# Exponentials as three shifted bit streams, and an inverse row transform by halves, in a spectral filter beside an attention

## The chip, the cores and the metric

The kernel runs on one core of a Trainium2 chip. Its engines are TensorE (PE; its weight loads are listed apart as PEld), VectorE (DVE), ScalarE (ACT), GpSimd (POOL) and the DMA queues, issued here by SyncE (SP). The metric is the device time of one execution in microseconds; the profile is of one execution.

## The reference

Two independent computations on a 2048 x 640 input each, whose outputs are put side by side. The first is a spectral filter: a two-dimensional real Fourier transform, a product with a complex weight, and the inverse transform. The second is a multi-head attention with 32 heads of width 20.

```python
def _A_ref(x, w_r, w_i):
    X = rfft2(x.astype(float32))
    X = X * (w_r + 1j * w_i)
    return irfft2(X, s=(S, D)).astype(bfloat16)

def _B_ref(x, wqkv, wo):          # H = 32, Dh = 20
    q, k, v = heads(x @ wqkv)
    p = softmax(einsum("bhqd,bhkd->bhqk", q, k) * Dh ** -0.5)
    o = einsum("bhqk,bhkd->bhqd", p, v)
    return merge(o) @ wo
```

All the times of this text belong to a program that does both. The scores of the attention are 32 x 2048 x 2048, and each needs an exponential; the filter is a chain of matrix products with tables of cosines and sines.

## The kernel before

The program is written by a scheduler of its own: at build time it plays the engines through with estimated durations, picks for each engine what to issue next, and emits fixed instruction streams. The engines then run in order and wait for each other on semaphores. So a change of one operation can move every instruction after it.

The scores are computed as tiles of 128 keys x 512 queries of one head (`score_mm`). Head width is 20, padded to 32 rows, so that up to four such matmuls, of four heads, run side by side in the array. There are 32 units (a query block and a group of four heads) of 64 tiles each. Most tiles go in pairs to ScalarE, which takes two PSUM banks in one instruction:

```python
self.put("act", lambda e: e.activation(o, in_, AF.Exp, bias=ACT_BIAS, scale=ACT_SCALE), ...)   # 128 x 1024
```

The others go to VectorE, which forms the exponential from the bits of a half-precision number. The scores come scaled so that 1024 steps are one power of two, with an offset in them. A first step per tile, clamping and converting to a 16-bit integer, frees the PSUM bank; three more steps run on four tiles at once.

```python
# p1, per tile: PSUM fp32 -> int16 (named L946 in the profile)
e.tensor_scalar(o, in_, 0.0, 31744.0, ALU.max, ALU.min)
...
# per batch of four tiles, on 2048 columns (L974, L975, L976)
e.tensor_scalar(Gu, Iu, 0x3FF, 0x3800, ALU.bitwise_and, ALU.bitwise_or)   # p2
e.tensor_tensor(Gf, If, Gf, ALU.mult)                                     # p3
e.tensor_scalar(Iu, Iu, 0x7C00, 0x0008, ALU.bitwise_and, ALU.bitwise_or)  # p4, in place
```

G and I, read as half-precision numbers, are two terms whose sum is the exponential, and TensorE adds them by multiplying both with the values. There are two such buffer pairs.

The value matmuls (`try_pv`, L1053) have 32 output rows, so four heads run side by side; a VectorE tile needs two of them, a ScalarE tile one. The filter's stages, S1 to S4, and the projections run between as background jobs, released by time between FT0 and FT1. `keep` matmuls are issued where TensorE would otherwise idle.

The eight PSUM banks: two pairs for ScalarE, four for everything else.

The inverse row transform (S3) before the change has four tables of 8 x 128 x 512, cosines and sines of two halves of the output rows, for even and odd frequencies:

```python
for idx in range(4):                 # h: half of the rows, par: even or odd frequencies
    h, par = divmod(idx, 2)
    for pl in range(2):
        for lt in range(3):
            for n in range(8):       # four cosine, four sine blocks
                e.matmul(o, l, self.tabs[b][:, n, :], start=(n == 0), stop=(n == 7))
            # one eviction, 128 x 512, to bf16
            e.tensor_scalar(Z[..., h * 512:(h + 1) * 512], ps, sc, None, ALU.mult)
```

The last stage (S4) multiplies Z with a table G, 192 matmuls of 320 columns, and writes sums and differences out.

Of the kernel before, what the change touches and what calls it, by code (L numbers as in the profile page):

```python
# [255 lines left out]
S = 2048  # L256
# [5 lines left out]
OFF = 15360.0  # L262
QSCALE = (DH ** -0.5) * math.log2(math.e) * 1024.0
LN2 = math.log(2.0)
PC = 1.50702
ACT_SCALE = LN2 / 1024.0
ACT_BIAS = math.log(PC) - 15.0 * LN2
SUM_MIN = 192.0
FBC = 322
UNITS = ([(qc, g) for g in range(4) for qc in range(2)] + [(0, g) for g in range(4, 8)] + [(1, g) for g in range(4, 8)]  # L270
# [4 lines left out]
class Job:  # L275
    def __init__(self, name, prio, pe=(), ev=(), after=(), rel=0.0, post=None):
        self.name = name
        self.prio = prio
        self.pe = list(pe)
        self.ev = list(ev)  # L280
        self.after = list(after)
        self.rel = rel
        self.post = post
        self.bank = None
        self.hold = 0
        self.rdy = []
        self.nxt = 0
        self.enx = 0
        self.done = False
        self.seq = 0  # L290
        self.need = []


class KB:
# [44 lines left out]
    def alloc(self):  # L339
# [11 lines left out]
        self.Gb = []  # L351
        for _ in range(2):
            self.i1_off = a.take(4096)
            self.Ib.append(a.bf(self.i1_off, 2048))
            self.Gb.append(a.bf(a.take(4096), 2048))
        self.Of = [a.f32(a.take(2048), 512) for _ in range(2)]
# [26 lines left out]
        assert self.zend - zB >= 24576 and self.zend - zD >= 5200, (self.zend - zB, self.zend - zD)  # L383
# [13 lines left out]
    def alloc_filter(self):  # L397
        a = self.ar
        zA, zB, zC, zD = self.zA, self.zB, self.zC, self.zD
        self.xf = [a.bf(zA + 10240 * i, 8 * 640).rearrange("p (t d) -> p t d", t=8) for i in range(2)]  # L400
        self.ftmp = [a.f32(zD + 2560 * i, 640) for i in range(2)]
        self.fx = [a.bf(o, 1280) for o in (zC + 13312, self.ob_off, self.wo_off)]
        self.xs = [self.nc.dram_tensor("xs%d" % i, (1024, 640), BF16, kind="Internal").ap() for i in range(2)]
        self.tabs = [a.bf(zC + 8192 * i, 8 * 512).rearrange("p (t k) -> p t k", t=8) for i in range(2)]
        self.X1 = a.bf(zB, 5 * 2 * 1024).rearrange("p (c r k) -> p c r k", c=5, r=2)
        self.Y = a.bf(zA, 8 * 4 * FBC).rearrange("p (c m l) -> p c m l", c=8, m=4)
        self.FD = a.bf(zC, 4 * 3 * FBC).rearrange("p (m t l) -> p m t l", m=4, t=3)
        o = zC + 4 * 3 * FBC * 2
        self.Wb = [[a.bf(o + (2 * i + s) * 2 * FBC * 2, 2 * FBC).rearrange("p (r l) -> p r l", r=2) for s in range(2)] for i in range(2)]
        self.Wx = [[a.bf(zA + 2576 + (2 * i + s) * 2 * FBC * 2, 2 * FBC).rearrange("p (r l) -> p r l", r=2) for s in range(2)] for i in range(2)]  # L410
        self.TU = a.bf(zD, 4 * FBC).rearrange("p (s r l) -> p s r l", s=2, r=2)
        self.VX = a.bf(zD + 8 * FBC, 4 * FBC).rearrange("p (s r l) -> p s r l", s=2, r=2)
        self.X24 = a.bf(zD + 16 * FBC, 8)
        self.Z = a.bf(zB, 3 * 4 * 1024).rearrange("p (t m s) -> p t m s", t=3, m=4)
        self.G = a.bf(zA, 3 * 2 * 640).rearrange("p (t m d) -> p t m d", t=3, m=2)
        self.outB += [a.bf(o, 640) for o in (zC + 5888, zC + 7168)]
        self.T1 = [a.f32(zA + 7680 + 1280 * i, 320) for i in range(2)]
        self.yo = [[a.bf(zA + 10240 + 2560 * i + 1280 * s, 640) for s in range(2)] for i in range(2)]
# [78 lines left out]
    def setup_B(self):  # L497
# [52 lines left out]
        off2 = float(np.uint32(0x44A044A0).view(np.float32))  # L550
# [410 lines left out]
    def close_batch(self):  # L961
        b = self.dbatch % 2
        tiles = self.dtiles
        n = len(tiles)
        self.dtiles = []
        self.dbatch += 1
        self.batches_open[b] = n * 2
        I_ = self.Ib[b][:, 0:n * 512]
        G_ = self.Gb[b][:, 0:n * 512]
        Iu, Gu = I_.bitcast(U16), G_.bitcast(U16)  # L970
        If, Gf = I_.bitcast(F16), G_.bitcast(F16)
        ik = [("I", b, i) for i in range(n)]
        ops = [
            (lambda e, en: e.tensor_scalar(Gu, Iu, 0x3FF, 0x3800, ALU.bitwise_and, ALU.bitwise_or), 100 + 0.26 * 512 * n, ik, [("G", b), ("G2", b)], [], "p2"),  # L974
            (lambda e, en: e.tensor_tensor(Gf, If, Gf, ALU.mult), 125 + 0.52 * 512 * n, ik + [("G", b)], [("G2", b)], [], "p3"),  # L975
            (lambda e, en: e.tensor_scalar(Iu, Iu, 0x7C00, 0x0008, ALU.bitwise_and, ALU.bitwise_or), 100 + 0.26 * 512 * n, [("G2", b)], ik, [], "p4"),  # L976
        ]

        def gdone():
            for i, t in enumerate(tiles):  # L980
                self.pv.append(dict(tile=t, src=self.Gb[b].bitcast(F16)[:, i * 512:(i + 1) * 512], key=("G2", b), last=False, b=b, bat=True, sid=1))
            for i, t in enumerate(tiles):
                self.pv.append(dict(tile=t, src=self.Ib[b].bitcast(F16)[:, i * 512:(i + 1) * 512], key=("I", b, i), last=True, b=b, bat=True, sid=2))
        bt = self.bat[self.dbatch - 1]

        def go():
            self.dve_push(ops, gdone, prio=self.PRP)
        bt[1] = (n, go)
        if bt[0] == n:
            go()  # L990
# [5 lines left out]
    def pv_waves(self, u):  # L996
# [7 lines left out]
        for (kt, sid), q in quads.items():  # L1004
            if len(q) == 4:
                ks = [it["key"] for it in q] + [("V", g // 2, kt), ("Vone",), ("Vpad",)]
# [4 lines left out]
    def try_pv(self, nmax=4):  # L1011
# [22 lines left out]
        for it in group:  # L1034
            uu, kt, j = it["tile"]
            rk += [it["key"], ("V", g // 2, kt)]
            hl = 4 * (g % 2) + j
            todo.append((self.V[:, kt, g // 2, hl * 21: hl * 21 + 32], it["src"], j, j not in st))
# [6 lines left out]
        if len(st) == len(group) and all(t[3] for t in todo):  # L1045
            wk, pwk = [("ps", bank)], []
        else:
            wk, pwk = [], [("ps", bank)]

# [215 lines left out]
    def eligible(self, J):  # L1265
# [5 lines left out]
        if J.need and not self.avail(J.need):  # L1271
            return False
# [344 lines left out]
    def filter_tables(self):  # L1617
# [14 lines left out]
        for h in range(2):  # L1632
            for par in range(2):
                k = 2 * np.arange(512, dtype=np.int64) + par
                sh = s[h * 512:(h + 1) * 512]
                ang = th * ((k[:, None] * sh[None, :]) % S)
                c_, n_ = np.cos(ang), np.sin(ang)
                if par == 0:
                    n_[0, :] = alt[h * 512:(h + 1) * 512]
                m = np.concatenate([c_.reshape(4, 128, 512), n_.reshape(4, 128, 512)], 0)  # L1640
                t3.append(m.transpose(1, 0, 2))
# [22 lines left out]
        g = np.stack([cl * np.cos(a4), cl * np.sin(a4)], 1)  # L1664
# [3 lines left out]
    def jobs_A(self, after, need):  # L1668
# [162 lines left out]
        hook("ldt3", S2, lambda: [load_t(self.tabs, self.c_t3, i, 3, "t3", [zr("C", 2)]) for i in range(2)])  # L1831
        S3 = []
        yk = [("Y", kc, m) for kc in range(9) for m in range(2)]
        for idx in range(4):
            h, par = divmod(idx, 2)
            b = idx % 2
            js = []
            for pl in range(2):
                zi = 2 * par + pl
                for lt in range(3):  # L1840
                    M = 128 if lt < 2 else 65
                    pe = []
                    for n in range(8):
                        m = (n // 4) * 3 if pl == 0 else 1 + n // 4

                        def mk(bank, n=n, m=m, lt=lt, M=M, b=b, par=par):
                            o = ps[0:M, bank, :]
                            l = self.Y[:, 4 * par + n % 4, m, lt * 128:lt * 128 + M]
                            r_ = self.tabs[b][:, n, :]
                            return lambda e: e.matmul(o, l, r_, start=(n == 0), stop=(n == 7))  # L1850
                        pe.append((mk, 216.0, yk + [("t3", idx), ("t3b", b), zr("A", 2), zr("C", 3)]))

                    def mkev(bank, zi=zi, lt=lt, M=M, h=h):
                        o = self.Z[0:M, lt, zi, h * 512:(h + 1) * 512]
                        in_ = ps[0:M, bank, :]
                        sc = -1.0 if zi % 2 == 1 else 1.0
                        return lambda e, en: e.tensor_scalar(o, in_, sc, None, ALU.mult)  # L1857
                    ev = [(mkev, 608.0, [zr("B", 2), zr("D", 3)], [("Z", lt, zi, h), zr("B", 1), zr("D", 2)], [], False)]
                    js.append(add(Job("S3", 0.0, pe, ev, after=S2)))
            S3 += js  # L1860
            if idx < 2:
                hook("ldt3_%d" % (idx + 2), js, (lambda idx: lambda: load_t(self.tabs, self.c_t3, idx + 2, 3, "t3", []))(idx))
        hook("ldwo", S3, lambda: [self.dma(self.woL[i][0:80, :], self.B_wo[480 + 80 * i:560 + 80 * i, :], 102400, w=[("woL", i), zr("C", 3)], name="ld_woL") for i in range(2)])
        hook("ldG", S3, lambda: self.dma(self.G.rearrange("p t m d -> p (t m d)"), self.c_G.ap(), 983040, w=[("G",), zr("A", 2)], name="ld_G"))
        for sc in range(8):
            for half in range(2):
                for T in range(2):
                    pe = []
                    for n in range(6):
# [8 lines left out]
                        ks = [("Z", lt, 2 * T + m, sc // 4), ("G",), zr("A", 3), zr("B", 2), zr("D", 3)]  # L1878
# [37 lines left out]
    FT1 = 760000.0  # L1916
# [210 lines left out]
```

## Time and profile before

| | |
|---|---|
| time, median of three | 794.51 us (794.4 to 799.35) |
| span of the profiled execution | 793.0 us |
| granted TensorE clock, mean | 0.999 of full speed |
| exponentials on ScalarE | 822 of two tiles |
| tiles on VectorE | 404 |
| data moved by DMA | 48.66 MB, 61 GB/s in the mean |

How to read it: the page gives each engine's busy time and its share of the span; a group line has the source line, engine and operation, what is written and read with shapes and count, then the busy time and the mean duration of one instruction, then the idle time just before them and what ended most of it. Busy times of overlapping instructions are merged, so count times mean can be more than the busy time. A window line gives the length, each engine's busy time with the number of instructions, the granted clock, the DMA share and GB/s. A timeline line gives start and length in us.

### The profile page before, as it was taken

The numbers are of one execution on the slowest core, as the hardware profiler recorded it, in microseconds if no ns is written. First come the engines' busy times: TensorE is split into PE (matmuls) and PEld (weight loads), VectorE is DVE, ScalarE is ACT, GpSimd is POOL, SyncE is SP. The second block draws the span as 40 slices with busy tenths as digits, with TensorE's granted clock in tenths as the row PEclk, the third lists the DMA queues.
The fourth block names the chain that finished last, engine by engine and source line by source line (L and its number), as shares of the span: only waits on it lengthen the run. The fifth ranks groups of instructions, "written<-read, shape, count | busy, mean of one in ns | idle before, by whom it ended". The sixth has DMA issues, their size and how long they took to land.

```text
span 793.0 us, 15248 instructions
## 1 busy us (share of the span) xinstructions
PE 751.3 (95%) x6115; PEld 235.1 (30%) x6115; DVE 699.7 (88%) x1077; ACT 764.6 (96%) x835; POOL 142.8 (18%) x141
## 2 busy tenths in 40 slices
PE   8999999999999999999999999999999999999897
PEld 4422333333222222223322332222222222332233
DVE  3698998988897888888999999899989998899996
ACT  5899999999999999999999999999999999999995
POOL 7396950000000012003022010001000100000000
PEclk9999999999999999999999999999999999999999
DMA  9023332021145212211011103010200112111101
GB/s 294 26 60 105 93 93 68 22 53 27 45 126 173 74 60 63 70 53 50 18 38 47 53 26 124 13 66 20 72 20 18 41 29 66 52 36 53 34 21 53
DMA packets 42861, 48.66 MB, mean 61 GB/s; under 512 B 16454, under 2 KB 36168, under 8 KB 41760
## 3 DMA queue, kind: packets, MB, share of 16 engines
q1 hardware_dynamic: 42016, 46.32, 19.4%
q0 software_dynamic: 768, 1.32, 0.6%
q8 instruction: 49, 0.80, 0.4%
q14 instruction: 28, 0.23, 0.1%
HBM read 32.53 MB, written 8.36 MB: 52 GB/s over the span
## 4 chain that ended last, share of the span: by engine, by line
ACT 65%; PE 24%; DVE 8%; DMA 1%; SPq 1%; issue 1%
ACT arena L1393 64%; PE ps L812 8%; PE ps L1053 5%; PE ps L634 3%; DVE arena L946 2%; DVE arena L975 2%; PE ps L605 2%; DVE arena L976 1%; DVE arena L974 1%; DMA arena<-ct 1%; PE ps L681 1%; PE ps L1762 1%; PE ps L1199 1%; SPq L471 1%; PE ps L1877 1%
## 5 line engine op out<-in xcount | busy, mean ns | idle before, releaser
L1393 ACT ACTIVATE arena<-ps 128x1024 f16<-128x1024 f32 x822 | 757.4, 1109 | 10.8 <-PE ps L812 8.3
L812 PE MATMUL ps<-arena 32*128 32x512 bf16 x2048 | 325.1, 384 | 27.6 <-ACT arena L1393 22.6
L946 DVE TENSOR_SCALAR arena<-ps 128x512 int16<-128x512 f32 x404 | 269.7, 683 | 44.7 <-PE ps L812 43.0
L1053 PE MATMUL ps<-arena 128*32 128x512 f16 x2452 | 192.4, 385 | 1.9 <-DVE arena L976 1.8
L812 PEld LDWEIGHTS ps<-arena 32*128 32x128 bf16 x2048 | 80.0, 91 | 325.9 <-ACT arena L1393 301.9
L1105 POOL TENSOR_TENSOR arena<-arena 128x512 bf16<-128x512 f32 x30 | 42.5, 1418 | 533.0 <-DMA arena<-rd 533.0
L975 DVE TENSOR_TENSOR arena<-arena 128x2048 f16<-128x2048 f16 x101 | 135.3, 1340 | 2.1
L974 DVE TENSOR_SCALAR arena<-arena 128x2048 uint16<-128x2048 uint16 x101 | 74.3, 735 | 1.7
L976 DVE TENSOR_SCALAR arena<-arena 128x2048 uint16<-128x2048 uint16 x101 | 75.6, 748 | 0.0
L1053 PEld LDWEIGHTS ps<-arena 128*32 128x32 bf16 x2452 | 40.5, 94 | 78.4 <-issue 59.3
L1850 PE MATMUL ps<-arena 128*128 128x512 bf16 (+1 forms) x192 | 56.3, 386 | 0.2 <-DVE arena L1857 0.2
L634 PE MATMUL ps<-arena 128*128 128x512 bf16 x170 | 49.8, 383 | 0.4 <-DVE arena L946 0.4
L1705 PE MATMUL ps<-arena 128*128 128x512 bf16 x160 | 46.7, 384 | 1.4 <-DMA arena<-ct 1.4
L1762 PE MATMUL ps<-arena 128*128 128x322 bf16 (+1 forms) x198 | 37.9, 304 | 1.3 <-DVE arena L1793 0.5
L1877 PE MATMUL ps<-arena 128*128 128x320 bf16 (+1 forms) x192 | 36.9, 303 | 0.1
L681 PE MATMUL ps<-arena 128*128 128x160 bf16 x320 | 31.5, 234 | 1.7 <-DVE arena L946 1.6
L1793 DVE TENSOR_TENSOR arena<-ps,arena 128x644 bf16<-128x644 f32 (+1 forms) x34 | 27.9, 820 | 1.0 <-PE ps L1762 0.6
L1199 PE MATMUL ps<-arena 128*128 128x320 bf16 (+1 forms) x152 | 28.6, 302 | 0.2 <-DVE arena L1857 0.2
L681 PEld LDWEIGHTS ps<-arena 128*128 128x128 bf16 x320 | 21.2, 98 | 14.7 <-issue 10.1
L646 DVE TENSOR_SCALAR arena<-ps 128x512 bf16<-128x512 f32 x34 | 23.2, 683 | 2.1 <-PE ps L634 2.1
L1084 DVE COPY arena<-ps 128x512 f32<-128x512 f32 (+1 forms) x33 | 22.0, 668 | 3.4 <-PE ps L1053 3.3
L687 DVE CAST arena<-ps 128x320 bf16<-128x320 f32 x32 | 15.5, 486 | 6.3 <-PE ps L681 6.3
(72 smaller groups left out, 364.2 us busy)
## 6 DMA issues: line engine op xcount, KB each, us to landing
arena<-ct SPq DMA_DIRECT2D x8, 1024.0 KB
arena<-rd SPq DMA_DIRECT2D x120, 64.0 KB
out_dram<-arena SPq DMA_DIRECT2D x32, 160.0 KB
arena<-arena SPq DMA_DIRECT2D x42, 80.0 KB
arena<-in_A_x_dram SPq DMA_DIRECT2D x16, 160.0 KB
xs<-arena SPq DMA_DIRECT2D x16, 160.0 KB
arena<-xs SPq DMA_DIRECT2D x2, 1280.0 KB
arena<-arena SPq DMA_DIRECT2D x105, 20.0 KB
```

Source lines behind the costliest of these rows:

```text
L634: return lambda e: e.matmul(o, l, r_, start=(cc == 0), stop=(cc == 4))
L681: return lambda e: e.matmul(o, l, r_, start=st, stop=(c == 4), skip_group_check=True)
L812: return e.matmul(self.ps[:, bank, :], self.KT[32 * j:32 * j + 32, g, kt * 128:(kt + 1) * 128], self.QT[32 * j:32 * j + 32, g, qc * 512:(q ...
L946: return e.tensor_scalar(o, in_, 0.0, 31744.0, ALU.max, ALU.min)
L974: (lambda e, en: e.tensor_scalar(Gu, Iu, 0x3FF, 0x3800, ALU.bitwise_and, ALU.bitwise_or), 100 + 0.26 * 512 * n, ik, [("G", b), ("G2", b)], ...
L975: (lambda e, en: e.tensor_tensor(Gf, If, Gf, ALU.mult), 125 + 0.52 * 512 * n, ik + [("G", b)], [("G2", b)], [], "p3"),
L976: (lambda e, en: e.tensor_scalar(Iu, Iu, 0x7C00, 0x0008, ALU.bitwise_and, ALU.bitwise_or), 100 + 0.26 * 512 * n, [("G2", b)], ik, [], "p4"),
L1053: inst = e.matmul(self.ps[32 * j:32 * j + 32, bank, :], v_, p_, start=s_, stop=False, tile_position=(0, 32 * j), skip_group_check=True)
L1393: self.put("act", lambda e: e.activation(o, in_, AF.Exp, bias=ACT_BIAS, scale=ACT_SCALE), 0.8333 * 512 * n + 60.0, r=[("ps", b) for b in b ...
L1705: return lambda e: e.matmul(o, l, r_, start=(t == 0), stop=(t == 7))
L1762: return lambda e: e.matmul(o, lhs, r_, start=st, stop=sp)
L1850: return lambda e: e.matmul(o, l, r_, start=(n == 0), stop=(n == 7))
```

## The change

It has two parts, and lets the scheduler move work.

First, VectorE's exponential. The two mask steps and the multiplication are replaced by two shifted and clamped copies of the same integer: G is max(I - 366, 0), and then I itself becomes max(I - 692, 0). With the first I there are three bit patterns; each is read as a half-precision number, which is linear between powers of two, and a weighted sum of three shifted ones comes nearer to the exponential. TensorE forms the sum: the first stream meets values scaled by 0.78125 (a small VectorE copy of 96 columns per batch, `Vs`), the other two the plain values. So a VectorE tile needs three value matmuls. The offsets and the scale of ScalarE's exponential move to match. The second subtraction overwrites I, and so waits until the first stream's matmuls have read it (the key `Ip`).

```diff
-OFF = 15360.0
+OFF = 14016.0
-PC = 1.50702
+PC = 2.27334
+SH1 = 366.0
+SH2 = 692.0
+W1 = 0.78125
...
-            (... e.tensor_scalar(Gu, Iu, 0x3FF, 0x3800, ALU.bitwise_and, ALU.bitwise_or), ..., "p2"),
-            (... e.tensor_tensor(Gf, If, Gf, ALU.mult), ..., "p3"),
-            (... e.tensor_scalar(Iu, Iu, 0x7C00, 0x0008, ALU.bitwise_and, ALU.bitwise_or), ..., "p4"),
+        pk = [("Ip", self.dbatch - 1, i) for i in range(n)]
+        def gdone():
+            push(self.Gb[b].bitcast(F16), [("G", b)] * n, 2)
+            self.dve_push([(... e.tensor_scalar(Ii, Ii, SH2, 0.0, ALU.subtract, ALU.max), occ, ik + pk, ik, [], "p3")],
+                          lambda: push(self.Ib[b].bitcast(F16), ik, 3), prio=self.PRP)
+        ops = [(... e.tensor_scalar(Gi, Ii, SH1, 0.0, ALU.subtract, ALU.max), occ, ik, [("G", b)], [], "p2")]
...
+        self.dve_push([(... e.tensor_scalar(vs, vi, W1, None, ALU.mult), 105.0, ..., "vs")], None, prio=self.PRP)
+        def go():
+            push(self.Ib[b].bitcast(F16), ik, 1, pk)
             self.dve_push(ops, gdone, prio=self.PRP)
```

Second, the inverse row transform. Cosine and sine parts are computed apart and for half of the rows only: row s is their sum, row 1024 - s their difference. Each pair of parts needs 4 + 4 matmuls for both halves, where 8 were needed for each half. The sine part is copied out first, then two additions read the cosine part in PSUM with the copy, one written in reverse order. The middle row and the highest frequency are handled by a small table `ex` and, for even frequencies, some extra matmuls: four or five of one column, and one of 512.

```diff
-                    for n in range(8):
-                        m = (n // 4) * 3 if pl == 0 else 1 + n // 4
-...
-                        return lambda e, en: e.tensor_scalar(o, in_, sc, None, ALU.mult)
+                    for sn in (1, 0):
+                        for n in range(4):
+                            pe.append((mm(4 * par + n, ms if sn else mc, t3[ti % 3][:, n, :], 0, 512, ...), 216.0, kt_))
+                        if par == 0:
+                            if sn:
+                                for n in range(4):
+                                    pe.append((mm(n, mc, self.ex[:, 512 + n:513 + n], 0, 1, False, False), 30.0, kx))
+                                pe.append((mm(0, ms, self.ex[:, 516:517], 0, 1, False, True), 30.0, kx))
+                            else:
+                                pe.append((mm(0, ms, self.ex[:, 0:512], 0, 512, False, True), 216.0, kx))
+                        if sn:   # copy out the sine part, and its middle row
+                            e.tensor_copy(sb[0:M, 1:512], ps[0:M, bank, 1:512])
+                            e.tensor_copy(Zt[:, 512:513], ps[0:M, bank, 0:1])
+                        else:    # sum, and difference in reverse
+                            e.tensor_tensor(Zt[:, 0:512], ps[0:M, bank, :], sb[0:M, :], ALU.add)
+                            e.tensor_tensor(Zt[:, 1023:512:-1], c_, s_, ALU.subtract)
...
-    FT1 = 760000.0
+    FT1 = 745000.0
```

There is one buffer for the sine part, and the S3 jobs are kept in order (`J.behind`). The tables are loaded in four pieces of 0.5 MB rather than four of 1 MB. The release of the filter's jobs is spread up to 745 and not 760 us of the scheduler's time. What it is for: VectorE's tiles get cheaper, so that more of the exponentials can go there, and TensorE is paid back in S3 for the third value matmul.

## The prediction

> **What bounds the kernel now.** I read the whole page first, for the shares and the chain, then ScalarE alone in windows of 50 us, then one stretch of the timeline, and last the start times of every instruction on TensorE.
>
> ```profile
> PE 751.3 (95%) x6115; PEld 235.1 (30%) x6115; DVE 699.7 (88%) x1077; ACT 764.6 (96%) x835; POOL 142.8 (18%) x141
> ...
> ACT 65%; PE 24%; DVE 8%; DMA 1%; SPq 1%; issue 1%
> ...
> L1393 ACT ACTIVATE arena<-ps 128x1024 f16<-128x1024 f32 x822 | 757.4, 1109 | 10.8 <-PE ps L812 8.3
> L812 PE MATMUL ps<-arena 32*128 32x512 bf16 x2048 | 325.1, 384 | 27.6 <-ACT arena L1393 22.6
> L946 DVE TENSOR_SCALAR arena<-ps 128x512 int16<-128x512 f32 x404 | 269.7, 683 | 44.7 <-PE ps L812 43.0
> L1053 PE MATMUL ps<-arena 128*32 128x512 f16 x2452 | 192.4, 385 | 1.9 <-DVE arena L976 1.8
> ...
> L975 DVE TENSOR_TENSOR arena<-arena 128x2048 f16<-128x2048 f16 x101 | 135.3, 1340 | 2.1
> L974 DVE TENSOR_SCALAR arena<-arena 128x2048 uint16<-128x2048 uint16 x101 | 74.3, 735 | 1.7
> L976 DVE TENSOR_SCALAR arena<-arena 128x2048 uint16<-128x2048 uint16 x101 | 75.6, 748 | 0.0
> ```
>
> Three engines are at 88 to 96%, and the chain of work that ended last is ScalarE for two thirds. The 2048 score tiles are shared out: 822 exponentials of two tiles each on ScalarE (1644 tiles) and 404 tiles on VectorE. ScalarE by window:
>
> ```profile
> 0.00:50.00 50.00, 32.71 (x35) 1.00 0.44 137
> ...
> 200.00:250.00 50.00, 48.57 (x54) 1.00 0.45 136
> ...
> 300.00:350.00 50.00, 50.00 (x56) 1.00 0.18 57
> ...
> 650.00:700.00 50.00, 48.20 (x53) 1.00 0.17 56
> ```
>
> From 50 us on it is hardly ever idle. One exponential is listed with 1109 ns, but they overlap: start to start the median is 904 ns. The first starts at 13.4 us, the last starts at 779.9 and ends at 781.1. So 821 steps x 0.904 = 742.2, and 766.5 - 742.2 = 24.3 us is all that ScalarE loses in between (6.4 of it before 100 us). After 781.1 come 11.9 us of tail to 793.0. The timeline shows what TensorE does meanwhile:
>
> ```profile
> 399.02 9.27 ACT L1393 ACTIVATE arena<-ps 128x1024 f16<-128x1024 f32 x10
> ...
> 401.92 0.39 PE L812 MATMUL ps<-arena 32*128 32x512 bf16 x2 [0.53 <-ACT arena L1393]
> ...
> 402.24 0.62 PE L1053 MATMUL ps<-arena 128*32 128x512 f16 x8
> ...
> 402.84 0.39 PE L812 MATMUL ps<-arena 32*128 32x512 bf16 x2
> ...
> 403.16 0.86 PE L1762 MATMUL ps<-arena 128*128 128x322 bf16 x5
> ...
> 403.96 0.39 PE L812 MATMUL ps<-arena 32*128 32x512 bf16 x3
> ```
>
> In every 0.904 us TensorE has to write one pair of score tiles (0.32 us to the next group's start, whether two or three tiles are written, as they run side by side) and may do one other thing: eight value matmuls (0.549 at the median), or some full-array ones. From the starts: a full-array matmul of 512 columns takes 216 ns, each change of group adds about 104, four value matmuls side by side take 216.
>
> [...]
>
> **The change part by part.** Counts are from the built programs' instruction orders.
>
> ScalarE: 784 exponentials, not 822; 480 tiles go to VectorE, not 404. 783 x 0.904 = 707.8, so 34.4 us less.
>
> VectorE: per batch of four tiles it loses the multiply (1340) and the two mask instructions (735, 748) and gets two subtract-and-clamp instructions on int16 of the same size, which I price as the masks, and a 128x96 scaling (about 190 ns, an estimate between the 128x16 and 128x128 tensor_scalar rows at 160 and 220). Removed: 101 x 2.823 = 285.1. Added: 120 x 1.673 = 200.8, and 76 first steps x 0.668 = 50.8. The inverse row transform: 24 evictions of 0.683 (16.4) become 12 copies (8.2), 12 one-column copies (2.3, estimated) and 24 two-input ones of about 0.681 (16.3; read between 480 ns for 320 and 820 for 644 elements). Sum -285.1 + 200.8 + 50.8 + 10.4 = -23: 677 us busy. VectorE gets lighter.
>
> TensorE: value matmuls go from 2452 to 3008, as a VectorE tile now needs three and not two: 139 more rounds of four x 0.216 = +30.0, and 67 more groups x 0.117 = +7.8. The inverse row transform goes from 192 full matmuls to 102 and 30 one-column ones: -90 x 0.216 + 30 x 0.06 = -17.6, and 28 groups fewer, -2.9. Score fills: 38 fewer x 0.216 and 11 groups fewer, -9.3. Keep-warm fillers, issued only when nothing else fits, 38 to 18: -5.5. Thirty matmuls of the last transform stage, and some group changes, move behind the attention: -5.6. Small groups: -1. Sum about -4. Added up with the same prices, all TensorE work between first and last fill was 706 us before, of the 768 there were; it will be 702.
>
> So ScalarE's need falls by 34 us and TensorE's by 4. Before, TensorE's work was 95% of ScalarE's 742; now it is 99% of 708. Each can be held up by the other: a late fill starves ScalarE, an unreleased bank stops TensorE. TensorE's 62 us of slack cannot all be given up, so I expect ScalarE's losses to grow from 24.3 us. Two places can be read from the order. Near the 200th exponential the new order has 4.8 us of TensorE work in one piece with no score fill (16 value matmuls and 51 value-projection matmuls of 160 columns, 69 ns each; the projections are late, and what waits for them holds the buffers): ScalarE has two sets in hand, 1.8 us, and some in flight, so about 3.7 us are lost. Cutting both orders into stretches of 14 fills, TensorE's work exceeds ScalarE's by 3.7 us in all before, by about 11 in the new one; less the 4.3 of that piece, some 3 more. For lateness that is handed on I add another 3. Losses: 24.3 + 3.7 + 6 = 34.
>
> Tail: the thirty 320-column matmuls now stand behind everything, 30 x 0.1365 = 4.1 us, so 11.9 becomes 16.
>
> Sum: 13.4 + 707.8 + 34 + 1.2 (last exponential) + 16 + 1.5 (median time over the traced span) = 774 us, 2.6% less.
>
> **The rivals.** (1) TensorE becomes the bound and its idle time does not shrink: 702 + 62 in place of 706 + 62, and the longer tail on top: about 794, no gain. For it: two of the three engines it must keep step with are as busy as before, and a quarter of the chain is already TensorE. Against: much of the 62 us is pairs of fills with nothing between them (36 groups of five or more tiles before, 16 in the new order), that is, waiting for ScalarE with no work to hand. (2) A new wait: the second subtract overwrites the buffer that the first stream's matmuls read, so VectorE, which ran its three steps without TensorE, now waits for it once per batch. At 0.3 us each that is 36 us of VectorE, 713 of 774; it could delay the banks, and make it 785 to 795. For it: in-order engines, both late. Against: two buffers, and the order puts other work between. [...] (4) Nothing grows but the visible piece: 765.
>
> **Range and chances.** The middle is 774. Rivals 1 and 2 in part pull up to 792, rival 4 down to 761. 2% faster is under 778.6, only 5 us above my middle: 0.62. Within 2%: 0.33. Slower by 2% needs rival 3 or a bad case of 2: 0.05.
>
> **What would show it.** Right: 784 exponentials at 904 ns; 480 first steps; both subtracts near 740 ns; an idle hole of ScalarE around the 200th exponential; its losses near 34 us in sum; TensorE's share of the chain up from 24% to 35% or more; after the last exponential some 16 us with the last stage's matmuls at the end. Wrong: subtracts above 1.2 us; VectorE waiting much on the value matmuls; ScalarE's losses at 45 us or more (then TensorE is the bound, rival 1) or still at 25 (rival 4).

## The result and the profile after

| | before | after |
|---|---|---|
| time, median | 794.69 us (794.4 to 799.35, four runs) | 767.27 us (765.67 to 769.53, four runs) |
| profiled execution: time, span | 794.8, 793.0 us | 769.5, 767.7 us |
| granted TensorE clock of it | 0.999 | 0.995 |
| exponentials on ScalarE | 822 | 784 |
| from the first one's start to the last one's start | 766.5 us | 736.4 us |
| tail after the last exponential | 11.9 us | 16.7 us |

The changed kernel takes 0.9647 of the time before (95% interval 0.9609 to 0.9684): 27 us, 3.5% less. A ratio leaves out runs more than 1.5% above the fastest of the same kernel: of all those below, two with the row transform alone, of 803.03 and 805.01 us. These lines of its page answer to those shown of before: the busy time of each engine, the chain of work that ended last, and the groups of instructions.

```profile
PE 734.2 (96%) x6532; PEld 237.0 (31%) x6591; DVE 669.4 (87%) x1234; ACT 729.5 (95%) x797; POOL 132.1 (17%) x142
...
ACT 65%; PE 26%; DVE 6%; DMA 1%; issue 1%; SPq 0%
...
L1418 ACT ACTIVATE arena<-ps 128x1024 f16<-128x1024 f32 x784 | 722.3, 1126 | 15.8 <-PE ps L821 12.3
L955 DVE TENSOR_SCALAR arena<-ps 128x512 int16<-128x512 f32 x480 | 320.5, 683 | 45.2 <-PE ps L821 43.0
L821 PE MATMUL ps<-arena 32*128 32x512 bf16 x2048 | 309.2, 385 | 13.4 <-ACT arena L1418 8.8
L1076 PE MATMUL ps<-arena 128*32 128x512 f16 x3008 | 236.0, 386 | 1.7 <-DVE arena L998 0.3
...
L998 DVE TENSOR_SCALAR arena<-arena 128x2048 int16<-128x2048 int16 x120 | 91.0, 758 | 1.4
L997 DVE TENSOR_SCALAR arena<-arena 128x2048 int16<-128x2048 int16 x120 | 86.7, 723 | 3.5 <-PE ps L1076 2.8
```

Compare with before: the exponentials are now L1418, the score tiles L821, VectorE's first step L955, the value matmuls L1076. L998 is the first subtraction and L997 the second; the three old steps are gone. The shares of the chain hardly moved. TensorE waited 8.8 us for ScalarE to release its banks where it had waited 22.6: part of the room for 556 more value matmuls came from there, part from the row transform. The second subtraction waited only 2.8 us for value matmuls.

ScalarE by window (length, busy time with the number of exponentials, granted clock, DMA share, GB/s):

```profile
50.00:100.00 50.00, 46.31 (x51) 0.98 0.28 81
100.00:150.00 50.00, 48.27 (x53) 0.95 0.24 65
...
200.00:250.00 50.00, 46.08 (x51) 1.00 0.18 42
...
300.00:350.00 50.00, 50.00 (x56) 1.00 0.16 51
...
500.00:550.00 50.00, 48.23 (x54) 1.00 0.18 58
```

Start to start the median exponential still takes 904 ns, so 783 steps are 707.8 us, and 736.4 - 707.8 = 28.6 us is what ScalarE lost in between (before: 24.3). The windows show where most of the new losses are: between 50 and 150 us, where the clock column is below one, between 200 and 250 us, and between 500 and 550 us; from 300 to 350 it is never idle. The one after 200 us is a single hole, here in the timeline (start, length, engine, line, what; in brackets the idle time before it and what ended it):

```profile
206.42 0.62 PE L1076 MATMUL ps<-arena 128*32 128x512 f16 x8
...
206.97 0.87 PE L690 MATMUL ps<-arena 128*128 128x160 bf16 x10
207.76 0.62 PE L1076 MATMUL ps<-arena 128*32 128x512 f16 x8
208.31 3.01 PE L690 MATMUL ps<-arena 128*128 128x160 bf16 x41
...
211.69 2.85 ACT L1418 ACTIVATE arena<-ps 128x1024 f16<-128x1024 f32 x3 [3.92 <-PE ps L821]
```

It is the 200th exponential. L690 are the value projections: 51 of them and 16 value matmuls, 4.8 us (from 206.42 to 211.26), with no score tile in between. ScalarE lost 4.2 us there, start to start.

The other loss is a period at half clock. The timeline around its start:

```profile
95.77 1.40 POOL L1630 TENSOR_TENSOR arena<-arena 128x640 f32<-128x640 bf16 x1
...
96.16 1.57 DVE L998 TENSOR_SCALAR arena<-arena 128x2048 int16<-128x2048 int16 x1
...
98.39 0.98 PE L690 MATMUL ps<-arena 128*128 128x160 bf16 x6 [1.10 <-DVE arena L955]
...
99.83 1.05 PE L1076 MATMUL ps<-arena 128*32 128x512 f16 x8
99.95 1.02 ACT L1418 ACTIVATE arena<-ps 128x1024 f16<-128x1024 f32 x1 [1.56 <-PE ps L821]
```

While GpSimd ran L1630, VectorE's subtraction took 1.57 us and not 0.70; the first step of a score tile (L955) and another eviction behind it came late, TensorE stood idle 1.10 us for them, and from then on eight value matmuls lasted 1.05 us and not 0.62 as beside the hole. TensorE in windows, the 3.41 us before and the 6.81 us after:

```profile
94.98:98.39 3.41, 2.05 (x20) 1.00 0.01 2
98.39:105.20 6.81, 6.81 (x44) 0.50 0.30 74
```

Five starts of ScalarE in a row, up to the one at 105.76, came late by 3.9 us in all. So of the 28.6 us, 4.2 are the hole, 3.9 the half clock, and 20.5 the rest, which is less than before's 24.3. Of this rest, 2.0 us are a second new hole, at the 521st exponential (505.8 to 508.7 us), which the prediction did not have. The two times are stable in different degree: the hole is in the instruction order, the half clock depends on the execution (the other three runs had clocks of 0.998 to 0.999 and were 1.9 to 3.9 us faster; a repetition below separates the two).

### The profile page after: what moved, and what is told of

Same layout as the page of the kernel before. It is cut to its first block, busy times and chain, and to the rows that moved or that the text cites. A ratio compares the mean times of both kernels' runs of the same rounds, so it can differ in the third digit from the quotient of the medians.

```text
span 767.7 us, 16364 instructions
## 1 busy us (share of the span) xinstructions
PE 734.2 (96%) x6532; PEld 237.0 (31%) x6591; DVE 669.4 (87%) x1234; ACT 729.5 (95%) x797; POOL 132.1 (17%) x142
## 4 chain that ended last, share of the span: by engine, by line
ACT 65%; PE 26%; DVE 6%; DMA 1%; issue 1%; SPq 0%
ACT arena L1418 65%; PE ps L821 8%; PE ps L1076 6%; DVE arena L955 2%; PE ps L1793 2%; PE ps L614 2%; PE ps L690 2%; PE ps L643 2%; PE ps L1222 1%; DVE arena L998 1%; PE ps L1896 1%; DMA arena<-ct 1%; DVE arena L997 1%; PE ps L1948 1%; PE ps L572 1%
## 5 line engine op out<-in xcount | busy, mean ns | idle before, releaser
L1418 ACT ACTIVATE arena<-ps 128x1024 f16<-128x1024 f32 x784 | 722.3, 1126 | 15.8 <-PE ps L821 12.3
L955 DVE TENSOR_SCALAR arena<-ps 128x512 int16<-128x512 f32 x480 | 320.5, 683 | 45.2 <-PE ps L821 43.0
L821 PE MATMUL ps<-arena 32*128 32x512 bf16 x2048 | 309.2, 385 | 13.4 <-ACT arena L1418 8.8
L1076 PE MATMUL ps<-arena 128*32 128x512 f16 x3008 | 236.0, 386 | 1.7 <-DVE arena L998 0.3
L821 PEld LDWEIGHTS ps<-arena 32*128 32x128 bf16 x2048 | 76.2, 91 | 297.4 <-ACT arena L1418 274.9
L998 DVE TENSOR_SCALAR arena<-arena 128x2048 int16<-128x2048 int16 x120 | 91.0, 758 | 1.4
L997 DVE TENSOR_SCALAR arena<-arena 128x2048 int16<-128x2048 int16 x120 | 86.7, 723 | 3.5 <-PE ps L1076 2.8
L1076 PEld LDWEIGHTS ps<-arena 128*32 128x32 bf16 x3008 | 50.5, 94 | 96.4 <-issue 65.9
L643 PE MATMUL ps<-arena 128*128 128x512 bf16 x149 | 44.8, 383 | 2.2 <-issue 1.7
L1736 PE MATMUL ps<-arena 128*128 128x512 bf16 x140 | 41.8, 383 | 3.4 <-issue 2.4
L1948 PE MATMUL ps<-arena 128*128 128x320 bf16 (+1 forms) x192 | 34.6, 302 | 0.0
L690 PE MATMUL ps<-arena 128*128 128x160 bf16 x320 | 31.3, 240 | 1.6 <-DVE arena L955 1.5
L1896 PE MATMUL ps<-arena 128*128 128x512 bf16 (+3 forms) x121 | 29.8, 332 | 2.1 <-issue 1.3
L1005 DVE TENSOR_SCALAR arena<-arena 128x96 bf16<-128x96 bf16 x120 | 29.3, 245 | 0.0
L690 PEld LDWEIGHTS ps<-arena 128*128 128x128 bf16 x320 | 22.3, 100 | 13.2 <-issue 10.4
L696 DVE CAST arena<-ps 128x320 bf16<-128x320 f32 x32 | 15.5, 488 | 11.9 <-PE ps L690 11.8
```

The source lines that it names most:

```text
L643: return lambda e: e.matmul(o, l, r_, start=(cc == 0), stop=(cc == 4))
L690: return lambda e: e.matmul(o, l, r_, start=st, stop=(c == 4), skip_group_check=True)
L821: return e.matmul(self.ps[:, bank, :], self.KT[32 * j:32 * j + 32, g, kt * 128:(kt + 1) * 128], self.QT[32 * j:32 * j + 32, g, qc * 512:(q ...
L955: return e.tensor_scalar(o, in_, 0.0, 31744.0, ALU.max, ALU.min)
L997: self.dve_push([(lambda e, en: e.tensor_scalar(Ii, Ii, SH2, 0.0, ALU.subtract, ALU.max), occ, ik + pk, ik, [], "p3")], lambda: push(self. ...
L998: ops = [(lambda e, en: e.tensor_scalar(Gi, Ii, SH1, 0.0, ALU.subtract, ALU.max), occ, ik, [("G", b)], [], "p2")]
```

## The experiments

Ten runs were made, each beside the kernel before, in three sets that share runs of before (medians 795.24, 794.75 and 794.69 us). My theory was that the streams give the gain by taking tiles from ScalarE, that S3 is worth nothing by itself and only makes room on TensorE, and that the changed kernel stands just where TensorE begins to hold ScalarE up.

### The streams without the new row transform

```diff
 # against the changed kernel
-                    for sn in (1, 0):      # S3 by halves: cosine and sine apart
-                        ...
+                    for n in range(8):     # S3 as before: 192 matmuls
+                        ...
-    FT1 = 745000.0
+    FT1 = 760000.0
```

> The three streams alone, with the inverse row transform as it was before. Theory A (ScalarE sets the pace, and TensorE work that finds no room beside it is pushed behind the last exponential, where it counts one for one): 778 exponentials, 777 x 0.904 = 702; losses about 25; 162 matmuls of the last filter stage now stand behind the attention, 22 us, so a tail near 34. 13.4 + 702 + 25 + 1.2 + 34 + 1.6 = 778 us. Theory B (the transform's savings lie off the path, as ScalarE is the bound, and could be left out): 760 us, with a tail near 17.

Measured: 777.69 us (776.93 to 777.93), ratio 0.9744 (0.9678 to 0.9809): faster, though the interval does not settle whether by 2%. ScalarE made 778 exponentials and lost 24.2 us, so the last one ended at 740.5, ten us earlier than in the changed kernel. But the tail is 34.6 us. The chain of this kernel, and then its timeline behind the attention:

```profile
PE 45%; ACT 43%; DVE 8%; DMA 2%; issue 1%; SPq 0%
```

```profile
747.88 22.26 PE L1896 MATMUL ps<-arena 128*128 128x320 bf16 x162
```

Here L1896 is the last filter stage: 162 of its 192 matmuls stand behind everything else. In the changed kernel it is 30. The 132 more at 0.1365 us are 18.0 us, and the tails differ by 17.9. So what TensorE could not fit in did not hold up the exponentials: it went to the end. The release of the filter's jobs up to 760 us, where the changed kernel has 745, plays no part: this kernel's instruction order is the same with either. Both new holes are in this kernel too (4.2 us at the 200th, 2.0 at the 521st): they come with the streams and not with S3.

### The row transform without the streams

```diff
 # against the changed kernel: the streams undone
-OFF = 14016.0
+OFF = 15360.0
-        ops = [(... e.tensor_scalar(Gi, Ii, SH1, 0.0, ALU.subtract, ALU.max) ..., "p2")]
+        ops = [(... bitwise_and, bitwise_or ..., "p2"), (... ALU.mult ..., "p3"), (... bitwise_and, bitwise_or ..., "p4")]
-        self.batches_open[b] = 3 * n
+        self.batches_open[b] = n * 2
-    FT1 = 745000.0
+    FT1 = 760000.0
```

> The new inverse row transform alone, with the exponentials as before. 824 exponentials. Theory A: TensorE has some 20 us less to do but nothing of it stood behind the attention before, so only ScalarE's losses can shrink a little: 13.4 + 744 + 22 + 1.2 + 12 + 1.6 = 794 us, between 789 and 797. Theory C (TensorE is a bound of its own beside ScalarE, and each us saved there is worth most of a us): 775 to 780.

Measured: 798.37 us (790.91 to 805.01, twenty runs), ratio 1.0015 (0.9986 to 1.0044). No gain: 824 exponentials, losses of 26.3 us, a tail of 10.8. The median lies just above the expected 789 to 797, which had no term for the clock. The spread is wide, and it follows the granted clock: two runs at 1.000 took 790.91 and 793.09, two at 0.981 took 801.80 and 801.84. The kernel before does the same: nine runs at 1.000 took 791.9 to 793.4, the one at 0.982 803.2. At full clock the two kernels can't be told apart. The profiled run (clock 0.989, 797.85 us) has its longest half-clock period at the same place as the changed kernel, and it begins in the same way: TensorE had waited 1.29 us for VectorE's first step. TensorE in the window of that period (busy time, number, clock):

```profile
96.38:106.60 10.22, 10.22 (x66) 0.50 0.15 45
```

So S3 alone buys nothing; with no matmul of the last stage behind the attention before (a tail of 11.9 us) there was nothing for it to bring forward.

### Two streams of three

```diff
-                self.pv.append(dict(..., last=sid == 3, ...))
+                self.pv.append(dict(..., last=sid == 2, ...))
-        self.batches_open[b] = 3 * n
+        self.batches_open[b] = 2 * n
-            self.dve_push([(... SH2, 0.0, ALU.subtract, ALU.max) ..., "p3")], lambda: push(self.Ib[b].bitcast(F16), ik, 3), ...)
+            self.dve_push([(... SH2, 0.0, ALU.subtract, ALU.max) ..., "p3")], None, ...)
```

This leaves the third stream out of the sum. VectorE still computes it; TensorE does not multiply it.

> The changed kernel without the value matmuls of the third stream: VectorE still makes it, TensorE leaves it out, so the output lacks one of the three terms. 782 exponentials, TensorE has about 29 us less to do. Theory A: the hole of ScalarE near the 200th exponential goes (4 us) and the tail keeps 24 of its 30 last-stage matmuls: 13.4 + 706 + 21 + 1.2 + 16 + 1.6 = 759 us, at least 755. Theory C: 767 - 29 x 0.8, about 744 or below.

Measured: 758.57 us (756.08 to 759.98), ratio 0.9509 (0.9444 to 0.9574). ScalarE's group on the page, with its idle time for score tiles (L821) at the end:

```profile
L1418 ACT ACTIVATE arena<-ps 128x1024 f16<-128x1024 f32 x782 | 719.6, 1122 | 6.6 <-PE ps L821 5.4 <-PE ps L1076 0.7
```

Waiting for score tiles went from 12.3 us to 5.4. With 2532 value matmuls in place of 3008 (119 rounds of four, 25.7 us of TensorE's work at 0.216, and some group changes) the time falls by 8.7 us only. ScalarE loses 18.5 us, start to start; both holes are gone, and in this execution (clock 0.998) so is the half clock; the tail is 14.8. Against the 20.5 us that were left of the changed kernel's losses without the first hole and the half clock, that is 2 us less, which is the size of the second hole. So no cost of TensorE's density that is spread over the exponentials can be told from zero here.

### Four streams

```diff
-        self.batches_open[b] = 3 * n
+        self.batches_open[b] = 4 * n
-            ... lambda: push(self.Ib[b].bitcast(F16), ik, 3), ...
+            ... lambda: (push(self.Ib[b].bitcast(F16), ik, 3), push(self.Ib[b].bitcast(F16), ik, 4)), ...
```

The last stream's end moves to the fourth as well (`last=sid == 4`). The third stream is multiplied twice, so the sum has one term too many.

> The changed kernel with the third stream multiplied twice, so the output has one term too many: TensorE gets about 27 us more, nothing else is added. 780 exponentials. Theory A: what does not fit goes behind the attention (174 last-stage matmuls, 24 us of tail) and into three long pieces without score fills of 6.1, 5.3 and 3.8 us: losses about 34, tail 36, 790 us. Theory B' (TensorE has slack, 39 us of it by my count, and takes the added work in): under 775. Together with the run that leaves a stream out: if A holds, taking 29 us from TensorE gives 8 or less and adding 27 costs 20 or more.

Measured: 795.53 us (794.0 to 799.12, twenty runs), ratio 1.0007 (0.9987 to 1.0027): the whole gain is gone. ScalarE made 780 exponentials and lost 39.4 us; the tail is 35.1, with 174 matmuls of the last stage in it. Of the 25 us between the two profiled runs, 18.4 are tail and 10.8 ScalarE's losses, against 4 exponentials fewer (3.6). And the losses are again holes, not a thin spread: 5.4, 4.5 and 5.3 us at single exponentials, 15.2 in sum, against one of 4.2; from 250 to 300 us, where the third stands, the mean clock is 0.93 as well (some 7 us at half clock, an estimate from that mean), and between 270 and 300 us another 4.5 us are lost. The expected 790 us had the tail right and the losses 5 us too low. The first of them in the timeline:

```profile
160.25 4.32 PE L690 MATMUL ps<-arena 128*128 128x160 bf16 x60
...
164.94 2.85 ACT L1418 ACTIVATE arena<-ps 128x1024 f16<-128x1024 f32 x3 [5.26 <-PE ps L821]
```

Sixty value projections in one piece. The two kernels together show the kink: 26 us of value matmuls less give 8.7, the 27 us more here (126 rounds) cost 28.

### Score tiles for VectorE only when it has little left to do

```diff
-    DVE_LOW = 1000.0
+    DVE_LOW = 600.0
```

The scheduler gives VectorE tiles by themselves, outside ScalarE's groups, only while VectorE's estimated backlog is below this many ns. The aim was to end the last stage inside the attention.

> The changed kernel with one number of its scheduler changed (VectorE tiles of their own are filled only while VectorE has under 0.6 us of work left, not 1.0). 784 exponentials as before and the same hole near the 200th, but 6 and not 30 matmuls of the last filter stage stand behind the attention. Theory A (what is left behind counts one for one): 24 x 0.1365 = 3.3 us less than 767.3, 764 us. Rival (the tail is set by the stores and the last attention output, and the matmuls fill its gaps): 767 to 768.

Measured: 763.51 us (763.01 to 764.77, six runs), ratio 0.9603 (0.9569 to 0.9636): 3.8 us under the changed kernel. From the end of its timeline:

```profile
755.40 0.98 PE L1948 MATMUL ps<-arena 128*128 128x320 bf16 x6
```

Only six matmuls of the last stage (L1948) stand behind, where the timeline of the changed kernel has thirty:

```profile
758.64 4.25 PE L1948 MATMUL ps<-arena 128*128 128x320 bf16 x30
```

The tail is 15.2 against 16.7. The exponentials are 784 in both, and the hole is the same (4.2 us, at 207.8). This kernel's six runs all had a clock of 0.998 or more; its losses of 24.4 less the hole are 20.2, so the rest is again what the changed kernel has without its half clock (20.5). Between the two profiled runs (6.4 us) 1.5 are the tail, 4.2 ScalarE's losses, nearly all of it the half clock, and 0.7 a first exponential that started earlier. So that the measured 763.5 us agrees with the expected 764 is luck: the 24 matmuls fewer took 1.5 us off the tail and not 3.3. The gain looked larger than what the edit explains, and both kernels were run again on one chip:

> The changed kernel once more, unchanged, to stand on the same chip as the other two of this set. Theory: its median is set by how often the half-clock period near 98 us occurs: runs with a granted clock of 0.998 or more take 765.5 to 767.7 us, those near 0.995 about 769.5; median near 767.

> The version with the backlog limit of 600 once more, beside the changed kernel on one chip. Theory: a shorter tail (1.5 us) and a first exponential that need not start earlier; at equal clock 1.5 to 2.5 us less than the changed kernel, the rest of the 3.8 us seen before being half-clock periods. Rival: the gain is all its own, 3.5 us or more at equal clock.

Measured: the changed kernel 765.91 us (765.3 to 769.75, six runs; ratio 0.9656, 0.9626 to 0.9687), the other 764.31 (762.96 to 765.01, six runs; ratio 0.9619, 0.9595 to 0.9644). The runs of the changed kernel fall into two groups: four at a clock of 0.998 or more took 765.3 to 766.4, two at 0.994 and 0.995 took 769.5 and 769.8. The half-clock period thus costs some 4 us, and it is there in some executions of one and the same kernel. At equal clock (the median of those four is 765.4, against 764.3) the edit is worth about 1 us, a little under the 1.5 of the tail and under the 1.5 to 2.5 expected; the rival, that all of the 3.8 is its own, falls. The profile of this second execution (clock 0.999) has no half-clock period: at its place TensorE waited 0.82 us for VectorE, not 1.10. ScalarE lost 25.1 us, 20.9 without the hole. And its chain reads differently, though no instruction moved:

```profile
ACT 59%; PE 34%; DVE 5%; DMA 1%; issue 0%; SPq 0%
```

### VectorE starts later

```diff
-    EARLY = 30000.0
+    EARLY = 60000.0
```

Until this time of the scheduler VectorE gets no score tiles. The late start was meant to let it share less with GpSimd, and TensorE do its projections earlier.

> The changed kernel with VectorE's exponentials starting at 60 and not at 30 us of the scheduler's time. In the order the piece of 4.8 us without score fills near the 200th exponential is gone, and so is one of 1.7 us near the 521st; 790 exponentials, not 784; 24 last-stage matmuls behind, not 30. Theory A: +6 x 0.904 = +5.4, -4.2 for the hole, -2.0 for the second, -0.8 of tail: 766 us, the same as the changed kernel. Rival (the hole is not caused by the third value matmul of early VectorE tiles, and only moves): 771 or more.

Measured: 767.24 us (766.48 to 768.83, six runs), ratio 0.9651 (0.9616 to 0.9686): the same as the changed kernel. ScalarE has 790 exponentials, 6 more (5.4 us), and loses 22.1 us. The hole at the 200th is gone, but a new loss took its place:

```profile
266.48 0.53 PE L1736 MATMUL ps<-arena 128*128 128x512 bf16 x1 [1.99 <-DMA arena<-ct]
...
267.59 1.02 ACT L1418 ACTIVATE arena<-ps 128x1024 f16<-128x1024 f32 x1 [2.04 <-PE ps L821]
```

TensorE waited 2 us for a table of the filter, and the first full-array matmul after it took 0.53 us where one took 0.38 elsewhere. Eight value matmuls took 1.05 us at 267.48 and at 270.09, as in the half clock of the changed kernel, and 0.61 again at 273.50. From 250 to 300 us ScalarE lost 5.4. The hole is not a law of the change: it is a place in one order, and a shift of the order trades it for another.

### Both, with a start in between

```diff
-    DVE_LOW = 1000.0
+    DVE_LOW = 600.0
-    EARLY = 30000.0
+    EARLY = 40000.0
```

> Backlog limit 600 and VectorE's start at 40 us of the scheduler's time. In its order the piece near the 200th exponential is gone (4.2 us), but there are 790 exponentials (5.4 us more) and 12 last-stage matmuls behind, not 6 (0.8 us). Theory: 763.5 - 4.2 + 5.4 + 0.8 = 765.5. Rival: without the piece nothing else collides, and it is the fastest of all: 762 or less.

Measured: 764.6 us (761.71 to 766.47, six runs), ratio 0.9622 (0.9594 to 0.965). The hole is gone, losses are 19.8 us, 12 matmuls of the last stage stand behind; but 790 exponentials take back what the hole gave. That is the version before (764.31) within the spread, and the rival (762 or less) falls.

### Larger pieces

```diff
-    DMIN = 14
+    DMIN = 18
-    DVE_LOW = 1000.0
+    DVE_LOW = 1500.0
-    VMIN = 8
+    VMIN = 12
```

VectorE takes tiles from a unit only while ScalarE has 18 left there, and value matmuls normally wait until three rounds of four are ready, not two: 361 groups of them in place of 391.

> The changed kernel with three numbers of its scheduler changed (fewest tiles left in a unit for VectorE to take one: 18, not 14; value matmuls wait for three rounds, 12 and not 8 tiles; own fills up to 1.5 us of VectorE work). 784 exponentials; one piece of 3.3 us without fills in place of those of 4.8 and 1.7; 3 last-stage matmuls behind, not 30. Theory A: hole 2.6 in place of 4.2, the second (2.0) gone, 3.7 less of tail: 767.3 - 7.3 = 760 us. Rival (values that wait for three rounds hold the buffers longer, and losses grow elsewhere): 765 or more.

A miss: 771.01 us (769.66 to 775.78, six runs), ratio 0.9714 (0.9673 to 0.9755). The parts that the instruction order shows came out as expected: 784 exponentials, a tail of 13.2, a hole of 2.5 us. What the order doesn't show did not: losses of 32.9 us. The worst of them:

```profile
263.60 0.25 DVE L1122 RECIPROCAL arena<-arena 128x16 f32<-128x16 f32 x1 [2.54 <-DMA arena<-sd]
...
264.45 0.40 PE L1076 MATMUL ps<-arena 128*32 128x512 f16 x4 [2.96 <-DVE arena L997]
...
265.29 2.11 ACT L1418 ACTIVATE arena<-ps 128x1024 f16<-128x1024 f32 x2 [2.42 <-PE ps L821]
```

A 128x16 reciprocal stands in VectorE's stream before the sums that it reads have come back from memory. All three engines wait in turn, and then the clock is halved (0.50 from 265.0 to 268.4). TensorE is slow a second time between 585.3 and 589.4: twelve value matmuls took 1.47 us at 587.47, where twelve took 0.83 at 98.00. Between 570 and 595 us ScalarE loses 3.8 us, where the second execution of the changed kernel loses 0.8. The rival's number (765 or more) came out; that values held the buffers longer, its reason, is not shown.

## Why the prediction was right, and where it was not

**ScalarE's share.** 784 exponentials at 904 ns: as predicted, and the bulk of the gain.

**VectorE.** The subtractions took 758 and 723 ns (predicted near 740), the scaling 245 (estimate 190; 178 at the median late in the run), VectorE in all 669 us (677). Rival 3, an int16 subtraction that takes above 1.2 us, was no more than an estimate of mine, and it falls: the subtraction is as fast as the masks were (735 and 748), though not early in the run. VectorE's windows for the first subtraction alone (length, then its busy time and number):

```profile
20.00:100.00 80.00, 13.29 (x10) 0.99 0.21 61
300.00:700.00 400.00, 47.06 (x67) 1.00 0.16 48
```

That is 1329 ns each against 702. It goes with GpSimd's work: GpSimd was busy 57.6 of these first 80 us and 42.9 of the 400 later. Over the whole run, the 100 first subtractions with no GpSimd instruction beside them took 0.65 to 0.70 us, the other 20 from 0.68 to 1.88. The first step, which reads PSUM, took 0.67 us in both windows.

**Rival 2, the new wait.** 2.8 us in sum against the 36 it needed: it falls.

**TensorE and ScalarE's losses: the step that failed.** The prediction put the losses at 34 us: before's 24.3, a hole of 3.7 near the 200th exponential, and 6 for density and lateness. The hole is there (4.2). The 6 us are not. Without the half clock, which I did not foresee, the losses are 24.7 with the hole in them, and 25.1 in the second execution: about before's 24.3, and at the 25 that the prediction named as the sign of rival 4. That the profiled run's 28.6 comes nearer to 34 is luck, 3.9 us of clock where I had put 6 of density. TensorE's work was 99% of ScalarE's by my count (with 60 ns for a one-column matmul of the row transform, an estimate; 22 of the 30 took 25 to 39 ns start to start), and I took that to thin out ScalarE's supply everywhere. The runs show that it doesn't: with two of three streams the losses shrink by the two holes and nothing more that can be told from zero, and four streams lose in holes, at half clock and in the tail. A score tile for ScalarE goes first in the scheduler's choice, and what does not fit is the background work; it is pushed along and appears behind the attention, or in one piece where its turn can't be put off any more. So the term to price was the length of the tail and of the largest pieces, not the density. The sign that I named for it, a share of TensorE in the chain of 35% or more, is a poor one: it was 26% in one execution of the changed kernel and 34% in the next. The chain follows whoever came last by a hair, and here two engines are level.

**Tail.** 16 predicted, 16.7 measured, with the 30 matmuls. The price of 0.1365 us for each is borne out for a long pile (132 of them, 17.9 of 18.0 us), not for a short one: with 6 behind, the tail was 15.2, with 24, 14.9 (the late start). So that 11.9 + 4.1 came out is partly luck.

**Rivals 1 and 4.** Rival 4 (only the visible piece grows: 765) was nearest to the 767.3 measured (765.9 in the repetition); had the 6 us been left out, the sum would have been 768. Rival 1 (TensorE holds all up, 794) is what four streams look like: 795.5. It was one term of work away, not wrong in kind.

**Clock.** The prediction had no term for it. In the profiled run it cost 3.9 us, in the repetition's runs some 4. It does not explain why the median of the changed kernel is 767.27 in one set and 765.91 in the other: the two middle runs of the first set (766.9 and 767.65) had a clock of 0.999.

**What each part gave.** By the medians the streams alone took 17.5 us off, S3 alone nothing, both 27.4. At a granted clock of 0.998 or more it is 793.3 us for before (13 runs of the first set), 777.7 for the streams alone and 765.4 to 766.9 for both (two sets), so the streams give some 15.6 and S3 on top of them 11 to 12. That S3 pays only with the streams is shown by the pair of runs; that it pays by taking 132 matmuls out of the tail is read from the traces (18 us less tail, 6 more exponentials and 4.4 us more losses against it).

**What stays open.** No run has a version without the hole that keeps 784 exponentials. And each edit moves the whole instruction order, so a small difference between two traces holds whatever else moved with it.

## What to carry to other kernels

Where a priority scheduler serves one engine first, extra work on the engine that feeds it does not slow the feed evenly: look at what is left behind at the end and at the largest uninterrupted pieces, and price those. A change that frees time on an engine that isn't the limit is worth nothing until another change uses that time, so run each part alone before judging either. And when two orders differ by a few us, look at the granted clock of each run first: in the changed kernel a wait of TensorE of 1.10 us came before a stretch at half clock that cost 3.9.

## What the runs showed of the hardware

The granted clock fell to 0.50 after short waits of TensorE: in the changed kernel for 6.8 us, after a wait of 1.10 us, in the one with S3 alone for 10.2, after 1.29, and in the retuned one for 3.4, behind a wait of 2.96. Neither the length of the wait nor TensorE's busy time ahead of it decides this alone. The kernel before waited 1.24 us at the same place and kept its clock, and up to the end of that wait its TensorE had been busy no longer than in the kernel with S3 alone. TensorE in the kernel before, in the stretch that ends with the wait and in the one after it (busy time, number, clock), and then the same with S3 alone:

```profile
92.50:95.97 3.47, 2.00 (x21) 1.00 0.54 116
95.97:106.00 10.03, 9.69 (x96) 1.00 0.15 45
```

```profile
92.90:96.38 3.48, 2.00 (x22) 1.00 0.52 112
96.38:106.60 10.22, 10.22 (x66) 0.50 0.15 45
```

In the changed kernel it was 2.05 of the 3.41 us. What does decide it is not shown by these runs.

The cost: with S3 alone the two runs at a mean clock of 0.981 took 9.8 us more than the two at 1.000. If the clock stood at 1.00 or 0.50 only, as in the stretches shown, a mean of 0.981 over 800 us is 30.4 us at half clock, an estimate; each us of it cost about a third of a us there, and in the changed kernel 6.8 us cost 3.9.
